# The first loads, warm-ups and last output tile of a gated mix of linear attention and a token MLP

## The chip, the core and the metric

The kernel runs on one core of one Trainium2 chip. A core has engines that run side by side, each with its own queue of instructions: TensorE (matmuls, PE in the profile; its weight loads are PEld), VectorE (DVE), ScalarE (ACT), GpSimd (POOL) and SyncE (SP), which here only issues DMAs. The metric is the device time of the kernel in microseconds (us).

## The reference, cut to what matters

```
x: 2048 x 512, 32 heads of 16; everything in bf16
g  = sigmoid(sum(x * gate_w))                     one number per token
q, k, v = x @ wqkv                                phi(t) = where(t > 0, t + 1, exp(t)) + 1e-6
kv = sum over tokens of phi(k) v^T                per head, and z = sum of phi(k)
a  = (phi(q) @ kv) / (phi(q) . z + 1e-6) @ wo
h  = layernorm(x)
u  = gelu(h^T @ w1 + b1)                          w1 mixes the 2048 tokens into 1792
b  = (u @ w2 + b2)^T
out = g * a + (1 - g) * b
```

## The kernel before, in words

The 2048 tokens are 16 tiles of 128 (`NT`), the 512 features 4 chunks of 128 (`ND`). `xs` holds x with tokens on partitions, `xT` holds it with features on partitions, `hs` the normalised x, `pk` phi of k, `pqT` phi of q transposed.

The order of instructions on each engine is the order in which the code is written (`manual_schedule`); a wait is placed where an instruction needs another's result. PSUM is used as eight banks, taken in turn (`bank`). The stages are:

1. Loads and warm-ups. SP issues most DMAs one after the other; ACT issues the first two loads of the k weights (`load_wk`). `load_x` brings a tile of x as it lies, `load_xT` brings tiles through the transposing DMA. Meanwhile `warm_up` runs matmuls on a constant.
2. The k loop. Tiles 0 and 1 (`HEADS`) are not loaded transposed: TensorE transposes them against an identity (`transpose_part`), VectorE or ScalarE copies the result into `xT` (`copy_part`), and then `k_part` multiplies them with Wk, chunk by chunk. From tile 2 on `xT` comes from the transposing loads. `k_phi` applies phi (ScalarE, then VectorE twice). Four tiles later (`LAG`) `g_tile` accumulates x^T phi(k) over all tokens, which needs the plain tile of x. `ln_step` takes a tile's mean and variance on VectorE.
3. The first three blocks of h^T w1, with the q blocks between; then the remaining blocks of u, with the small matrices of the attention and the normalisers beside them.
4. The output loop: for each tile a product for the attention (`aps`), fourteen for the MLP (`yps`), the sum on VectorE and a store. The last tile is cut into pieces of columns, so that its first stores can leave early.

In stage 2 TensorE's order for the first two tiles is this:

```
for t in range(HEADS):
    for k0, k1 in ((0, 1), (1, 2), (2, ND)):
        transpose_part(t, k0, k1)
        copy_part(t, k0, k1, (t, k0) in ((0, 2), (1, 1)))
    k_part(0, range(2) if t == 0 else (2,))
k_part(1, range(2))
k_part(0, (3,))
```

All matmuls pass through the helper `mm`, so they share line 110; the tiles' names tell them apart: `wps` warm-ups, `pt` transposes, `kacc` k_part, `gacc` g_tile, `yps` the output. `load_x` is line 126, `load_wk` line 129, `load_xT` line 132, `ln_step` lines 233 and 234, the sum of the output line 501 and its store line 505.

Of the kernel before, what the change touches and what calls it, by code (L numbers as in the profile page):

```python
# [15 lines left out]
def kernel(  # L16
# [13 lines left out]
    nc = tc.nc  # L30
    P = nc.NUM_PARTITIONS
# [4 lines left out]
    X = A_x.flatten_outer_dims()  # L36
    O = out.flatten_outer_dims()
    S, D = X.shape
    F = B_w1.shape[1]
    NT = S // P  # L40
# [25 lines left out]
    def keep(shape, dtype, name):  # L66
        return persist.tile(shape, dtype, name=name, tag=name)

    def bank(name, dtype=FP32):
        return ps.tile([P, SC], dtype, name=name, tag="bank")  # L70

    xs = keep([P, NT, D], BF16, "xs")
    hs = keep([P, NT, D], BF16, "hs")
# [16 lines left out]
    ident = keep([P, P], BF16, "ident")  # L90
# [18 lines left out]
    def mm(o, lhsT, rhs, start, stop, **kw):  # L109
        nc.tensor.matmul(o, lhsT=lhsT, rhs=rhs, start=start, stop=stop, **kw)  # L110
# [14 lines left out]
    def load_x(q, t0, n):  # L125
        q.dma_start(out=xs[:, t0 : t0 + n, :], in_=x_view[:, t0 : t0 + n, :])

    def load_wk(q, k, n):
        q.dma_start(out=wk_sb[:, k : k + n, :], in_=wqkv_view[:, k : k + n, D : 2 * D])

    def load_xT(t0, n):
        nc.sync.dma_start(
            out=xT[:, :, t0 * P : (t0 + n) * P], in_=X[t0 * P : (t0 + n) * P, :], transpose=True
        )

    load_x(nc.sync, 0, 1)
    load_wk(nc.scalar, 0, 2)
    load_x(nc.sync, 1, 1)
    load_wk(nc.scalar, 2, 1)
    load_wk(nc.sync, 3, 1)  # L140
    for t in (2, 3, 4):
        load_xT(t, 1)
    nc.vector.memset(ones_f[:], 1.0)
# [3 lines left out]
        out=ident[:], in_=ident[:], compare_op=ALU.not_equal, fill=1.0, base=0,  # L147
# [5 lines left out]
        out=maskQ[:], in_=maskH[:].rearrange("p (a m) -> p m a", m=2), op=ALU.max, axis=AX.X  # L153
    )
    nc.gpsimd.memset(brow[:], 0.0)

    load_xT(5, 2)
    load_x(nc.sync, 2, 2)
    load_xT(7, 3)
# [15 lines left out]
    def load_small():  # L175
        nc.gpsimd.dma_start(out=brow[0:NF, :], in_=B_b1.rearrange("(f q) -> f q", q=P))
        nc.gpsimd.dma_start(out=brow[NF : NF + NT, :], in_=B_b2.rearrange("(f q) -> f q", q=P))
        nc.gpsimd.dma_start(
            out=gw_b[:], in_=gate_w.rearrange("(o d) -> o d", o=1).to_broadcast([P, D])
        )  # L180
# [3 lines left out]
    def warm_up(n, cols=SC):  # L184
        for _ in range(n):
            mm(wps[:, :cols], warm[:, 0:P], warm[:, :cols], True, True)

    act_warm = keep([P, 1], FP32, "act_warm")
    nc.scalar.activation(out=act_warm[:], in_=ones_f[:], func=ACT.Exp)
    warm_up(6)  # L190

    pts = {}

    def transpose_part(t, k0, k1):
        pt = pts[t, k0, k1] = bank("pt")
        for k in range(k0, k1):
            mm(pt[:, k * P : (k + 1) * P], xs[:, t, k * P : (k + 1) * P], ident[:], True, True)

    def copy_part(t, k0, k1, on_act):
        src = pts.pop((t, k0, k1))[:, k0 * P : k1 * P].rearrange("p (k s) -> p k s", k=k1 - k0)  # L200
        dst = xT[:, k0:k1, t * P : (t + 1) * P]
        if on_act:
            nc.scalar.activation(out=dst, in_=src, func=ACT.Copy)
        else:
            nc.vector.tensor_copy(out=dst, in_=src)  # L205
# [13 lines left out]
    def k_part(t, ks):  # L219
        if t not in kaccs:  # L220
            kaccs[t] = bank("kacc")
        for k in ks:
            mm(
                kaccs[t][:], xT[:, k, t * P : (t + 1) * P], wk_sb[:, k, :],
                k == 0, k == ND - 1,
            )

    def k_phi(t):
        phi(pk[:, t, :], kaccs.pop(t))

    def ln_stats(t):
        stats = work.tile([P, nc.vector.BN_STATS_DIM], FP32, name="stats", tag="stats", bufs=2)
        nc.vector.bn_stats(out=stats[:], in_=xs[:, t, :])  # L233
        nc.vector.bn_aggr(out=mv[:, t, :], in_=stats[:])  # L234

    def ln_rstd(g):
        s = slice(g * TPC, (g + 1) * TPC)
        nc.vector.tensor_scalar_add(out=veps[:, s], in0=mv[:, s, 1], scalar1=EPS)
        nc.gpsimd.tensor_tensor(out=rstd[:, s], in0=veps[:, s], in1=mhalf[:], op=ALU.pow)

    def ln_shift(g):
        s = slice(g * TPC, (g + 1) * TPC)
        nc.vector.scalar_tensor_tensor(  # L243
            out=nmr[:, s], in0=mv[:, s, 0], scalar=-1.0, in1=rstd[:, s],
            op0=ALU.mult, op1=ALU.mult,
        )

    def ln_apply(t):
        nc.scalar.activation(  # L249
            out=hs[:, t, :], in_=xs[:, t, :], func=ACT.Identity,  # L250
            scale=rstd[:, t : t + 1], bias=nmr[:, t : t + 1],
        )
# [3 lines left out]
    def g_tile(t):  # L256
        if not gacc:
            gacc.extend(bank("gacc") for _ in range(ND))
        for k in range(ND):
            mm(gacc[k][:], xs[:, t, k * P : (k + 1) * P], pk[:, t, :], t == 0, t == NT - 1)  # L260
# [15 lines left out]
    def ln_step(u):  # L276
        ln_stats(u)
        if u % TPC == TPC - 1:
            ln_rstd(u // TPC)
# [9 lines left out]
    k_phi(0)  # L289
    k_part(1, range(2, ND))  # L290
    k_phi(1)
    ln_step(0)
    ln_step(1)
    LAG = 4
    LN_LAG = 5
    APPLY = 10
    for t in range(HEADS, NT):
        k_part(t, range(ND))
        k_phi(t)
        if t >= LAG:  # L300
            g_tile(t - LAG)
        if t > LN_LAG + 1:
            ln_step(t - LN_LAG)
        if t == TPC - 1 + LN_LAG:
            load_small()
        if t >= APPLY:
            ln_apply(t - APPLY)
        if t in (TPC + LN_LAG, 2 * TPC + LN_LAG):
            ln_shift((t - LN_LAG) // TPC - 1)
# [73 lines left out]
    def den_block(c, j):  # L383
        seg = pqT[:, j, c * SC : (c + 1) * SC]
        pz = work.tile([P, SC], FP32, name="pz", tag="pz", bufs=2)
        nc.scalar.activation(out=pz[:], in_=seg, func=ACT.Copy, scale=zcol[:, j : j + 1])  # L386
        nc.vector.transpose(out=zT[:], in_=pz[:])  # L387
        den = work.tile([P, SC // HEAD], FP32, name="den", tag="den", bufs=1)
        nc.vector.tensor_reduce(  # L389
            out=den[:], in_=zT[:].rearrange("p (a d) -> p a d", d=HEAD), op=ALU.add, axis=AX.X  # L390
        )
        rd = work.tile([P, SC // HEAD], BF16, name="rd", tag="rd", bufs=1)
        with nc.allow_low_precision(reason="the normalizer is used in bf16"):
            nc.vector.reciprocal(out=rd[:], in_=den[:])
        rex = work.tile([P, SC], BF16, name="rex", tag="rex", bufs=1)
        nc.vector.transpose(  # L396
            out=rex[:].rearrange("p (a d) -> p a d", d=HEAD),
            in_=rd[:].unsqueeze(2).to_broadcast([P, SC // HEAD, HEAD]),
        )
        nc.vector.tensor_tensor(out=seg, in0=seg, in1=rex[:], op=ALU.mult)  # L400
# [42 lines left out]
    for j in range(NB0, NF):  # L443
        c, jj = divmod(j, FB)
        i = j - NB0
        acc = bank("uacc")
        for t in range(NT):
            if i == 2 and t < BRIDGE:
                for q in range(0, P, Q32):
                    c0 = jj * P + q  # L450
# [24 lines left out]
        out=gg[:], in0=gth[:], scalar1=0.5, scalar2=0.5, op0=ALU.mult, op1=ALU.add  # L475
    )
    nc.vector.tensor_scalar(
        out=c1[:], in0=gth[:], scalar1=-0.5, scalar2=0.5, op0=ALU.mult, op1=ALU.add
# [3 lines left out]
    for t in range(NT):  # L482
        c, tl = divmod(t, TPC)
        aps = bank("aps")
        for j in range(ND):
            mm(aps[:], pqT[:, j, t * P : (t + 1) * P], W2sb[:, j, :], j == 0, j == ND - 1)
        a_sc = work.tile([P, D], FP32, name="a_sc", tag="a_sc", bufs=2)
        nc.scalar.activation(  # L488
            out=a_sc[:], in_=aps[:], func=ACT.Identity,
            scale=gg[:, t : t + 1], bias=c2[:, t : t + 1],  # L490
        )
        for c0, W in ((0, 2 * P), (2 * P, P), (3 * P, P)) if t == NT - 1 else ((0, D),):
            cs = slice(c0, c0 + W)
            yps = bank("yps")
            for f in range(NF):
                mm(
                    yps[:, :W], w2c[c][:, f, tl * P : (tl + 1) * P], uT[:, f, cs],
                    f == 0, f == NF - 1,
                )
            ot = opool.tile([P, D], BF16, name="ot", tag="ot")  # L500
            nc.vector.scalar_tensor_tensor(  # L501
                out=ot[:, :W], in0=yps[:, :W], scalar=c1[:, t : t + 1], in1=a_sc[:, cs],
                op0=ALU.mult, op1=ALU.add,
            )
            (nc.scalar if t < 2 else nc.sync).dma_start(out=o_view[:, t, cs], in_=ot[:, :W])
        if t < NSC * ND - NDB:
            den_block(*divmod(t + NDB, ND))
# [30 lines left out]
```

## Time and profile before

| | us |
|---|---|
| median of 3 runs | 162.76 (162.43 to 162.89) |
| time of the profiled execution | 162.26 |
| its span, first to last instruction | 160.6 |
| TensorE busy | 155.9 |
| VectorE busy | 124.3 |
| ScalarE busy | 72.7 |

The profile is one execution. Its span lies inside its time; the rest is start and end of the launch. A line of the timeline has the start in us from the span's start, the duration in us, the engine, the line of the code and what is written from what; a letter q behind an engine's name means that the engine issued a DMA. The chain is followed back from the last instruction to what released it, and printed in order of time. A matmul's end is modelled, and neighbouring matmuls overlap in the records; the starts are what to compare. The granted clock of TensorE is 1.00 for the whole span.

### The profile page before, as it was taken

To read this page: it belongs to the slowest core of one execution; us is meant where nothing else is said; L and a number is where in the kernel's file an instruction comes from. 1 tells how busy PE (TensorE), PEld (TensorE's weight loads), DVE (VectorE), ACT (ScalarE), POOL (GpSimd) and SP (SyncE) were. 2 spreads that over 40 slices of the span, in tenths; PEclk is the share of its full clock that TensorE was granted. 3 is DMA by queue.
4 is the path that set the end of the run, shared out by engine and by line. 5 is a ranking of instruction groups with operands and counts; after the bars stand their busy time and mean duration, and the time that the engine had idled before them with its cause. 6 is when DMAs were issued, how large, how long until landed. Compare 5 with 4: busy or idle time off the path is not lost.

```text
span 160.6 us, 2228 instructions
## 1 busy us (share of the span) xinstructions
PE 155.9 (97%) x822; PEld 72.5 (45%) x836; DVE 124.3 (77%) x274; ACT 72.7 (45%) x113; POOL 7.3 (5%) x17
## 2 busy tenths in 40 slices
PE   7999999999999999999999999999999999999993
PEld 2444444444444445444444444444444444444462
DVE  1599999769999998756999999676999999711122
ACT  3543486654978393059873320237333442111110
POOL 3000332002010000000000000000000000000000
PEclk9999999999999999999999999999999999999999
DMA  5699999999970007600930679401000001110001
GB/s 168 150 231 262 328 352 329 354 349 348 336 171 0 0 0 257 204 0 4 356 101 2 213 244 306 151 33 37 33 33 33 33 33 58 48 61 33 33 33 33
DMA packets 29929, 23.07 MB, mean 144 GB/s; under 512 B 8384, under 2 KB 29888, under 8 KB 29920
## 3 DMA queue, kind: packets, MB, share of 16 engines
q1 hardware_dynamic: 29104, 22.15, 45.2%
q10 hardware_dynamic: 704, 0.66, 1.2%
q0 software_dynamic: 112, 0.14, 0.4%
q8 instruction: 6, 0.10, 0.3%
q14 instruction: 3, 0.02, 0.0%
HBM read 19.01 MB, written 2.10 MB: 131 GB/s over the span
## 4 chain that ended last, share of the span: by engine, by line
PE 84%; DVE 13%; issue 1%; ACT 0%
PE yps L110 30%; PE uacc L110 24%; PE kacc L110 9%; PE gacc L110 9%; PE aps L110 9%; DVE pqT L213 6%; DVE zacc L274 3%; DVE stats L233 2%; DVE e L210 2%; PE wps L110 2%; PE qacc L110 1%; DVE mv L234 1%; ACT e L209 0%; PE kvps L110 0%; PE w2ps L110 0%
## 5 line engine op out<-in xcount | busy, mean ns | idle before, releaser
L110 PE MATMUL uacc<-hs,w1c 128*128 128x512 bf16 (+1 forms) x227 | 50.8, 379 | 0.4 <-issue 0.2
L110 PE MATMUL yps<-uT,w2c 128*128 128x512 bf16 (+2 forms) x247 | 50.8, 355 | 0.3
L110 PEld LDWEIGHTS <-w2c 128*128 128x128 bf16 x252 | 23.6, 98 | 25.2
L110 PEld LDWEIGHTS <-w1c 128*128 128x128 bf16 (+1 forms) x233 | 21.8, 98 | 26.0 <-issue 0.2
L488 ACT ACTIVATE a_sc<-aps,c,gg 128x512 f32<-128x512 f32 x16 | 12.4, 775 | 31.2 <-PE aps L110 15.5
L501 DVE SCALAR_TENSOR_TENSOR ot<-yps,c,a_sc 128x512 bf16<-128x512 f32 (+2 forms) x18 | 12.3, 688 | 15.3 <-PE yps L110 11.7
L322 ACT ACTIVATE uT<-uacc,bcol 128x512 bf16<-128x512 f32 x14 | 9.3, 686 | 17.5 <-PE uacc L110 17.4
L110 PE MATMUL qacc<-xT,wq_sb 128*128 128x512 bf16 x64 | 16.4, 379 | 0.1
L110 PE MATMUL aps<-W2sb,pqT 128*128 128x512 bf16 x63 | 16.4, 379 | 0.1
L110 PE MATMUL kacc<-wk_sb,xT 128*128 128x512 bf16 x63 | 15.9, 379 | 0.2 <-DVE xT L205 0.2
L387 DVE STREAM_TRANSPOSE zT<-pz 128x512 f32<-128x512 f32 x16 | 11.3, 705 | 6.0 <-ACT pz L386 6.0
L110 PE MATMUL gacc<-pk,xs 128*128 128x512 bf16 x63 | 15.7, 379 | 0.1
L249 ACT ACTIVATE hs<-xs,nmr,rstd 128x512 bf16<-128x512 bf16 x16 | 12.8, 805 | 2.3 <-DVE nmr L243 2.3
L209 ACT ACTIVATE e<-kacc 128x512 bf16<-128x512 f32 x16 | 9.4, 594 | 9.7 <-PE kacc L110 8.5
L386 ACT ACTIVATE pz<-pqT,zcol 128x512 f32<-128x512 bf16 x16 | 11.4, 715 | 4.8 <-DVE ot L501 4.7
L209 ACT ACTIVATE e<-qacc 128x512 bf16<-128x512 f32 x16 | 9.5, 594 | 7.7 <-PE qacc L110 7.7
L396 DVE STREAM_TRANSPOSE rex<-rd 128x512 bf16<-128x512 bf16 x16 | 11.4, 711 | 0.6
L213 DVE SCALAR_TENSOR_TENSOR pqT<-qacc,e 128x512 bf16<-128x512 f32 x16 | 11.1, 692 | 0.6
L213 DVE SCALAR_TENSOR_TENSOR pk<-kacc,e 128x512 bf16<-128x512 f32 x16 | 11.1, 692 | 0.6
L389 DVE TENSOR_REDUCE den<-zT 128x32 f32<-128x512 f32 x16 | 11.0, 686 | 0.6
L210 DVE TENSOR_SCALAR e<-e 128x512 bf16<-128x512 bf16 x32 | 9.0, 282 | 2.5 <-ACT e L209 2.5
L233 DVE BATCH_NORM_STATS2 stats<-xs 128x6 f32<-128x512 bf16 x16 | 10.9, 683 | 0.0
(58 smaller groups left out, 96.2 us busy)
## 6 DMA issues: line engine op xcount, KB each, us to landing
w2c<-in_B_w_dram SPq DMA_DIRECT2D x8, 896.0 KB, 5.7
w1c<-in_B_w_dram SPq DMA_DIRECT2D x3, 2048.0 KB, 14.0
out_dram<-ot SPq DMA_DIRECT2D x13, 128.0 KB, 1.7
xs<-in_A_x_dram SPq DMA_DIRECT2D x1, 1024.0 KB, 6.6
w1c<-in_B_w_dram SPq DMA_DIRECT2D x1, 1024.0 KB, 15.3
xs<-in_A_x_dram SPq DMA_DIRECT2D x1, 512.0 KB, 5.0
wq_sb<-in_A_wqkv_dram SPq DMA_DIRECT2D x1, 512.0 KB, 5.6
wv_sb<-in_A_wqkv_dram SPq DMA_DIRECT2D x1, 512.0 KB, 12.3
```

Of the source, the lines that this page charges most:

```text
L110: nc.tensor.matmul(o, lhsT=lhsT, rhs=rhs, start=start, stop=stop, **kw)
L209: nc.scalar.activation(out=e[:], in_=acc[:], func=ACT.Exp)
L210: nc.vector.tensor_scalar(out=e[:], in0=e[:], scalar1=1.0, scalar2=PHI_EPS, op0=ALU.min, op1=ALU.add)
L213: nc.vector.scalar_tensor_tensor(out=dst, in0=acc[:], scalar=0.0, in1=e[:], op0=ALU.max, op1=ALU.add)
L233: nc.vector.bn_stats(out=stats[:], in_=xs[:, t, :])
L249: nc.scalar.activation(out=hs[:, t, :], in_=xs[:, t, :], func=ACT.Identity, scale=rstd[:, t : t + 1], bias=nmr[:, t : t + 1],)
L386: nc.scalar.activation(out=pz[:], in_=seg, func=ACT.Copy, scale=zcol[:, j : j + 1])
L387: nc.vector.transpose(out=zT[:], in_=pz[:])
L389: nc.vector.tensor_reduce(out=den[:], in_=zT[:].rearrange("p (a d) -> p a d", d=HEAD), op=ALU.add, axis=AX.X)
L396: nc.vector.transpose(out=rex[:].rearrange("p (a d) -> p a d", d=HEAD), in_=rd[:].unsqueeze(2).to_broadcast([P, SC // HEAD, HEAD]),)
L488: nc.scalar.activation(out=a_sc[:], in_=aps[:], func=ACT.Identity, scale=gg[:, t : t + 1], bias=c2[:, t : t + 1],)
L501: nc.vector.scalar_tensor_tensor(out=ot[:, :W], in0=yps[:, :W], scalar=c1[:, t : t + 1], in1=a_sc[:, cs], op0=ALU.mult, op1=ALU.add,)
```

## The change

The first tile of x for the transposes is loaded as 64 partitions with two consecutive tokens each (rows of 2 KB) into a corner of `hs` that is not used until later. It is transposed in eight products 64 wide, one for each chunk and each of the two tokens, and `copy_part` puts the two interleaved halves in place. The plain load of tile 0, which `g_tile` and `ln_step` need, is issued on SP after three transposing loads, and `ln_step(0)` moves behind tile 5 of the k loop. Of the Wk loads, chunks 1 and 2 go first on ACT, chunk 0 second on SP, chunk 3 second on ACT; tile 1 of x is the third load of SP. The warm-ups are four matmuls of 512 columns and one of 384 instead of six of 512. The last output tile is cut into 384 and 128 columns instead of 256, 128 and 128.

```diff
-    load_x(nc.sync, 0, 1)
-    load_wk(nc.scalar, 0, 2)
+    xp = hs[: P // 2, 0:2, :]
+    nc.sync.dma_start(out=xp, in_=X[0:P, :].rearrange("(p i) d -> p i d", i=2))
+    load_wk(nc.scalar, 1, 2)
+    load_wk(nc.sync, 0, 1)
+    load_wk(nc.scalar, 3, 1)
     load_x(nc.sync, 1, 1)
-    load_wk(nc.scalar, 2, 1)
-    load_wk(nc.sync, 3, 1)
     for t in (2, 3, 4):
         load_xT(t, 1)
...
+    load_x(nc.sync, 0, 1)
     load_xT(5, 2)
...
-    warm_up(6)
+    warm_up(4)
+    warm_up(1, 384)
...
         for k in range(k0, k1):
-            mm(pt[:, k * P : (k + 1) * P], xs[:, t, k * P : (k + 1) * P], ident[:], True, True)
+            if t == 0:
+                for i in range(2):
+                    c = k * P + i * (P // 2)
+                    mm(
+                        pt[:, c : c + P // 2], xp[:, i, k * P : (k + 1) * P],
+                        ident[: P // 2, : P // 2], True, True,
+                    )
+            else:
+                mm(pt[:, k * P : (k + 1) * P], xs[:, t, k * P : (k + 1) * P], ident[:], True, True)
...
+        if t == 0:
+            src = src.rearrange("p k (i s) -> p k i s", i=2)
+            dst = dst.rearrange("p k (s i) -> p k i s", i=2)
...
-    ln_step(0)
     ln_step(1)
...
+        if t == LN_LAG:
+            ln_step(0)
...
-        for c0, W in ((0, 2 * P), (2 * P, P), (3 * P, P)) if t == NT - 1 else ((0, D),):
+        for c0, W in ((0, 3 * P), (3 * P, P)) if t == NT - 1 else ((0, D),):
```

## The prediction

> **What bounds the kernel now.** I read the page first, then the chain that ended last, then the first ten microseconds on each queue and engine.
>
> ```profile
> span 160.6 us, 2228 instructions
> PE 155.9 (97%) x822; PEld 72.5 (45%) x836; DVE 124.3 (77%) x274; ACT 72.7 (45%) x113; POOL 7.3 (5%) x17
> ...
> PE 84%; DVE 13%; issue 1%; ACT 0%
> ```
>
> TensorE is busy for 97% of the span. The chain, in order of time, shows where it isn't:
>
> ```profile
> 0.85 2.72 PE wps L110 x6
> ...
> 4.06 0.60 PE kacc L110 x2
> 4.66 0.22 PE pt L110 x4
> 4.89 0.22 PE kacc L110
> 5.10 0.00 issue
> 5.11 3.84 PE kacc L110 x17
> 8.95 0.86 PE gacc L110 x4
> ...
> 154.69 3.10 PE yps L110 x42
> ```
>
> From 5.11 us to the last matmul at 157.8 us TensorE has no hole worth naming (the VectorE stretch of the chain from 33.8 to 55.5 us runs level with it). So whatever moves that 5.11 moves the end by as much, and beyond it only the tail counts. What sets the 5.11 is seen in the loads of the first microseconds (source, queue, KB, us from issue to landing, each issue asked for by itself):
>
> ```profile
> wk_sb<-in_A_wqkv_dram ACTq DMA_DIRECT2D x1, 256.0 KB, 3.1
> xs<-in_A_x_dram SPq DMA_DIRECT2D x1, 128.0 KB, 2.3
> ...
> xs<-in_A_x_dram SPq DMA_DIRECT2D x1, 128.0 KB, 3.0
> wk_sb<-in_A_wqkv_dram ACTq DMA_DIRECT2D x1, 128.0 KB, 3.3
> ...
> wk_sb<-in_A_wqkv_dram SPq DMA_DIRECT2D x1, 128.0 KB, 3.3
> ```
>
> SP issues at 0.81, 1.27 and 1.73, ACT at 0.81 and 1.30. Issue plus landing gives five slots: first SP load 3.1, first ACT load 3.9, second SP load 4.3, second ACT load 4.6, third SP load 5.0. They land in the order of issue, 0.3 to 0.8 apart. The DMA engines' share in steps of 0.5 us says why:
>
> ```profile
> 1.80:2.30 0.50, 0.50 (x3) 0.16 (x2) 0.16 (x1) 0.48 (x1) 0.38 (x2) 1.00 0.54 147
> 2.30:2.80 0.50, 0.50 (x2) 0.15 (x1) 0.00 (x0) 0.50 (x1) 0.00 (x0) 1.00 0.87 287
> 2.80:3.30 0.50, 0.50 (x2) 0.10 (x1) 0.00 (x0) 0.49 (x2) 0.00 (x0) 1.00 1.07 373
> ```
>
> (The last two columns are the DMA share and GB/s.) From 2.8 us the 16 engines are full. The front is a queue of 768 KB through a full pipe, and the order in it is what the change alters.
>
> **The change, part by part.**
>
> *The order of the first loads.* Before, the slots carry x tile 0, Wk chunks 0 and 1, x tile 1, Wk chunk 2, Wk chunk 3. After, they carry x tile 0, Wk 1 and 2, Wk 0, Wk 3, x tile 1. The bytes in each slot are the same; x tile 1 goes from the third slot (4.3) to the fifth (5.0), Wk 0 from the second (3.9) to the third (4.3). TensorE's order is kept: two k_part products of tile 0, then the four transposes of tile 1, then the rest. So Wk 3, now early, gains nothing: its product stands behind the transposes of tile 1, and so does everything else on TensorE. Wk 0 at 4.3 lets the two products run from 4.3 to about 4.75 instead of 4.06 to 4.5, which ends before x tile 1 is there. What decides is x tile 1. Today its weights load at 4.32 and its transposes start at 4.50, when the two products are through:
>
> ```profile
> 4.32 0.39 PEld L110 LDWEIGHTS <-xs 128*128 128x128 bf16 x4
> 4.50 0.39 PE L110 MATMUL pt<-ident,xs 128*128 128x128 bf16 x4
> ```
>
> After, they start at landing plus 0.05. Bounds of that landing: no x load before came sooner than 2.3 after its issue, so 1.73 + 2.3 = 4.03 at the least; the fifth slot as it is, 5.04; and 5.3 if the new first load takes 0.3 longer. I take 5.0, since the queue in front of it holds the same 640 KB. Slip: 5.05 - 4.50 = 0.55 us, with ends of -0.4 and +0.85. The steps behind the transposes (copies, products) are the same, so 5.11 becomes about 5.66.
>
> *The first tile as 64 rows of 2 KB.* The trace has no such load. It can help by at most what the engines leave idle between 1.8 and 2.8: 0.46 x 0.5 + 0.13 x 0.5 = 0.30 us, which would bring every slot forward by as much (x tile 1 at 4.74, slip 0.29). It can hurt by 0.3, if half the partitions draw on half the engines (147 GB/s at a share of 0.54 is that picture). I take about 0.05 of gain, already in the 5.0. The Trainium skill, "SBUF — State Buffer", section "Door 1: The DMA port swizzle", speaks against this part: partitions 0 to 63 reach only 8 of the 16 DMA ports, about 218 GB/s instead of 436. An estimate from that page is 0.3 us more for these 128 KB; the sum below would then be 0.8 instead of 0.5.
>
> *Its transposes and copies.* Eight products 64 wide instead of four 128 wide, and copies that write every second column. Today 0.87 us pass from the weight load at 3.19 to the first k_part product at 4.06. Even with x tile 0 no earlier and four more transposes at the 0.13 of today's slow ones (0.53 for 4), that makes 3.19 + 0.87 + 0.53 = 4.59 and the two products end at 5.03. The cover is x tile 1 at 5.05; if that came at 4.74, up to 0.25 would show.
>
> *Warm-ups.* 4.75 instead of 6 matmuls of 0.45 (2.72 / 6): 0.57 us off TensorE before 3.6 us, where it would wait for loads anyway. Gain zero. The risk is the rate: warm-ups go at 0.45 us each, the k_part products at 0.226 (3.84 / 17), and the step falls between 3.6 and 4.1 us after some 2.8 us of unbroken work. The granted clock in the rows says 1.00 on both sides, so only durations show it. After the change TensorE pauses twice before 5 us. I take no cost; the far end is five products and four transposes at the slow rate, 5 x 0.22 + 4 x 0.05 = 1.3 us. The Trainium skill, "TensorE: Matmul & The Clock Gate", Part 1, ties the rate to about 3.4 us of sustained activity; by that rule the thinned front would run slow for longer, and as an estimate the sum would be nearer 1.
>
> *The plain load of tile 0, now on SP behind three transposing loads.* It takes the issue place at 6.16, and costs SP the 0.42 of a like issue plus a gap, so all later SP loads go 0.45 later. First in line is the transposing load for tiles 5 and 6:
>
> ```profile
> 6.16 1.30 SPq L132 DMA_TRANSPOSE xT<-in_A_x_dram  x1
> ...
> xT<-in_A_x_dram SPq DMA_TRANSPOSE x1, 3.1
> ...
> 8.57 0.75 PEld L110 LDWEIGHTS <-xs 128*128 128x128 bf16 x4
> 9.43 0.74 PEld L110 LDWEIGHTS <-xT 128*128 128x128 bf16 x4
> ```
>
> It lands at 6.16 + 3.1 = 9.26 and its first weight load is at 9.43: 0.17 of slack. After: 6.61 + 3.1 = 9.71, against 9.43 + 0.55 = 9.98, so it hides under the slip, with 0.27 to spare. But it is a floor: if x tile 1 came early, this load would hold TensorE at a slip of 0.3 all the same. The plain tile itself is wanted by g_tile(0), at 8.57 + 0.55 = 9.12; it lands at 6.16 + 2.3 = 8.46, at worst 6.16 + 3.3 = 9.46, 0.34 late. I take the former, as the queue has drained by then. Behind these, tiles 2 and 3 of x (issue 7.50, landing 3.0 later, wanted at 12.02) and the rest have over half a microsecond to spare.
>
> *ln_step(0) moved* from before phi of tile 2 to behind phi of tile 5: one bn_stats and bn_aggr, 0.68 + 0.18. VectorE works through from 6.59 to 14.76 and meets its input again only at tile 7 (14.79), so the pair is done within the same stretch. Zero; 0.86 if it ended after that point.
>
> *The tail.* 28 instead of 42 matmuls for the same 7168 columns. 42 take 3.10, 14 of 512 columns take 3.02, so an extra matmul costs 0.003: 14 fewer save 0.04. The sum of the 384 wide piece on VectorE is near 0.62 (0.484 at 256, 0.752 at 512) and starts 0.78 before the last piece is ready; its store is issued before the last one. The last 128 columns and their store are as before.
>
> **Sum:** +0.55 - 0.04 = +0.51 us on the profiled execution's 162.26, so 162.77. The median of the runs shown, 162.76, lies 0.5 above that profile, so the same sum on the median is 163.3 us.
>
> **Rivals.** (1) Not slower: the 2 KB rows land so much sooner that all slots move up. The place is x tile 1, the price 0.3: landing at 4.74, slip 0.29, then the floor of the tiles 5 and 6 load at 0.3. That gives 163.0. It decides if x tile 1 lands before 4.95. For it: the idle DMA share at 1.8 to 2.8. Against: the pipe is full from 2.8 on.
> (2) The matmul rate stays low into the dense stretch: 0.4 to 1.3 more, 163.7 to 164.6. For it: 1.25 warm-ups fewer and two pauses. Against: the step came well before 5 us, and most of the work ahead of it remains.
> (3) Faster: SP's loads don't queue behind ACT's, and x tile 1 lands near 4.03. Then the load for tiles 5 and 6 holds TensorE unless it, too, lands in 2.7 (the shortest transposing load seen), at 9.3: slip -0.1, 162.6. Against: the five slots land in strict order today.
>
> **How the numbers follow.** A difference of 0.3% (0.49 us) is about what a measurement tells from no change. Main case 0.50, with slips of 0.4 to 0.85 (163.1 to 163.6), about a third of it under 0.49; rival (1) 0.25; rival (2) 0.15; rival (3) 0.10, partly within 0.3%. So slower 0.53, same 0.40, faster 0.07. The range 162.6 to 164.1 goes from rival (3) to the low half of rival (2).
>
> **What would show it.** The chain's dense k_part stretch starts near 5.65 instead of 5.11; the weight load of x tile 1 waits for its DMA to about 5.0; the load for tiles 5 and 6 lands near 9.7, with no wait there; the last stretch on TensorE falls by 0.04. I am wrong if x tile 1 lands before 4.5, if the weight load for tile 5 or for g_tile(0) waits long, or if k_part products after 5.6 take 0.4 us.

## The result and the profile after

The changed kernel takes 181.51 us (median of 5 runs, 181.31 to 182.16), the kernel before 162.53 us. The ratio is 1.117, with a 95% interval of 1.115 to 1.120. The forecast was 163.3 us: the direction came true, the size and the cause were missed. The profiled execution took 182.16 us.

The page after, its span, engines and chain:

```profile
span 180.4 us, 2206 instructions
...
PE 157.6 (87%) x811; PEld 72.1 (40%) x825; DVE 124.3 (69%) x273; ACT 72.8 (40%) x113; POOL 7.3 (4%) x17
...
PE 86%; SPq 7%; DMA 4%; issue 1%; DVE 0%; DVEq 0%
```

The work is nearly the same, TensorE 157.6 us against 155.9; its share fell from 97% to 87%. Two owners are new in the chain: SP's queue and the DMAs. In order of time (start, duration in us):

```profile
11.14 2.72 SPq L132
...
14.54 7.49 DMA xT<-in_A_x_dram
...
22.15 0.31 DVE xT L219
...
22.51 0.61 PE kacc L110
23.12 0.43 PE pt L110 x4
23.55 5.24 PE kacc L110 x18
```

The k_part stretch that began at 5.11 us begins at 23.55. Ahead of it stands a copy on VectorE (line 219, `copy_part`), and ahead of the copy a DMA into `xT` that was issued at 14.54 and landed at 22.03. That is the load of tiles 13 to 15, the last of the seven transposing loads. The table of waits names the two copies that stood still, and TensorE behind them (total, times, longest):

```profile
ACT xT L217 <- DMA xT<-in_A_x_dram: 18.8, 1, 18.8
...
DVE xT L219 <- DMA xT<-in_A_x_dram: 16.5, 1, 16.5
PE kacc L110 <- DVE xT L219: 16.2, 1, 16.2
```

These copies write tile 0 of `xT`; the loads write tiles 2 to 15. No element is shared. The copy of chunk 0 didn't wait, only those of the later chunks. The front of the timeline shows that, and a second surprise:

```profile
0.81 1.00 ACTq L129 DMA_DIRECT2D wk_sb<-in_A_wqkv_dram  x2
...
0.81 0.58 SPq L137 DMA_DIRECT2D hs<-in_A_x_dram  x1
...
5.01 0.44 PEld L110 LDWEIGHTS <-hs 64*128 64x128 bf16 x8 [2.79 <-DMA hs<-in_A_x_dram]
5.02 0.60 PE L110 MATMUL pt<-ident,hs 64*128 64x64 bf16 x8 [1.99 <-DMA hs<-in_A_x_dram]
5.34 0.30 DVE L219 CAST xT<-pt 128x128 bf16<-128x128 f32 x1 [3.10 <-PE pt L110]
```

The first tile as 64 rows of 2 KB was ready for TensorE at 5.0 us, where the tile of 128 rows had been at 3.19. Its issue on SP took 0.58 us, where the load before took 0.40.

### The profile page after: what moved, and what is told of

Same layout as the page of the kernel before. It is cut to its first block, busy times and chain, and to the rows that moved or that the text cites. A ratio compares the mean times of both kernels' runs of the same rounds, so it can differ in the third digit from the quotient of the medians.

```text
span 180.4 us, 2206 instructions
## 1 busy us (share of the span) xinstructions
PE 157.6 (87%) x811; PEld 72.1 (40%) x825; DVE 124.3 (69%) x273; ACT 72.8 (40%) x113; POOL 7.3 (4%) x17
## 4 chain that ended last, share of the span: by engine, by line
PE 86%; SPq 7%; DMA 4%; issue 1%; DVE 0%; DVEq 0%
PE uacc L110 27%; PE yps L110 27%; PE kacc L110 8%; PE gacc L110 8%; PE aps L110 8%; PE qacc L110 7%; SPq L132 5%; DMA xT<-in_A_x_dram 4%; SPq L126 2%; PE kvps L110 0%; SPq L137 0%; SPq L129 0%; PE pt L110 0%; PE w2ps L110 0%; DVE ot L516 0%
## 5 line engine op out<-in xcount | busy, mean ns | idle before, releaser
L110 PEld LDWEIGHTS <-w2c 128*128 128x128 bf16 x238 | 22.8, 98 | 25.9
L110 PE MATMUL kacc<-wk_sb,xT 128*128 128x512 bf16 x62 | 17.7, 413 | 16.3 <-DVE xT L219 16.2
L110 PEld LDWEIGHTS <-xT 128*128 128x128 bf16 x64 | 6.7, 104 | 25.0 <-DVE xT L219 17.2
L219 DVE CAST xT<-pt 128x128 bf16<-128x128 f32 (+1 forms) x4 | 1.3, 330 | 20.5 <-DMA xT<-in_A_x_dram 16.5
## 6 DMA issues: line engine op xcount, KB each, us to landing
w1c<-in_B_w_dram SPq DMA_DIRECT2D x3, 2048.0 KB, 13.5
```

## The experiments

The leading theory after the result: the copies of tile 0 wait for the transposing loads because their destination is now written as a split pattern (even and odd columns). The rival: the new loads and their order starve TensorE, and the wait is a sign of that. The smaller parts of the change were then measured one by one. Each ratio below is to the kernel before on the same chip, with its 95% interval. Each trace is of one execution.

**e1: the changed kernel without the split destination.**

```diff
-                    c = k * P + i * (P // 2)
-                    mm(pt[:, c : c + P // 2], xp[:, i, ...], ident[: P // 2, : P // 2], True, True)
+                    po = pt[:, k * P : (k + 1) * P].rearrange("p (s i) -> p i s", i=2)
+                    mm(po[:, i, :], xp[:, i, ...], ident[: P // 2, : P // 2], True, True)
...
-        if t == 0:
-            src = src.rearrange("p k (i s) -> p k i s", i=2)
-            dst = dst.rearrange("p k (s i) -> p k i s", i=2)
```

> The changed kernel, with one thing undone: the two halves of tile 0 are put in place by the transposing matmuls (every second column of PSUM) instead of by the copies, whose destination in xT is then one plain run per chunk, as before. Theory (the copies of chunks 1 to 3 wait for the transposing loads of tiles 5 to 15 because of the way their destination is written): that wait goes, TensorE's dense stretch starts near 6.5 us instead of 23.5, and the time is 163.5 to 165.5 us, the rest over 162.5 being the first tile's late landing (4.97 us in the changed kernel) and some slow matmuls. Rival (the first loads themselves, the 64 rows of 2 KB and their order, starve TensorE): little changes, over 175 us.

Measured: 166.15 us (165.05 to 166.69), ratio 1.022 (1.019 to 1.024). Its chain from the start:

```profile
0.81 4.03 DMA hs<-in_A_x_dram
4.83 0.05 issue
4.88 1.03 PE pt L110 x8
5.91 0.97 PE kacc L110 x2
6.88 0.43 PE pt L110 x4
7.30 4.32 PE kacc L110 x18
```

The wait is gone, and 15.4 of the 19.0 us with it. The 3.4 us that remain begin with the load of the first tile, 4.03 us from issue to landing. They are a little over the theory's range. Part of them is the price of this edit itself: the same eight products took 0.60 us in the changed kernel, where each writes 64 neighbouring PSUM columns, and take 1.03 here, where each writes every second one. The matmul rate was low in both.

**e2: the kernel before with the split pattern alone.**

```diff
         dst = xT[:, k0:k1, t * P : (t + 1) * P]
+        if t == 0:
+            src = src.rearrange("p k (s i) -> p k i s", i=2)
+            dst = dst.rearrange("p k (s i) -> p k i s", i=2)
```

> The kernel before, with one thing added: the copies of tile 0 name source and destination as even and odd columns, so that the same numbers go to the same places through a split pattern. Loads, warm-ups, transposes and tail are those of before. Theory (the split destination alone brings the wait): the second copy waits until the load for tiles 13 to 15 lands, near 21.8 us in the profile before, and the time is 179 to 182 us. Rival (the loads are the cause): 162.5 to 163 us.

Measured: 180.42 us (2 runs), ratio 1.109 (1.104 to 1.113). The same numbers go to the same places, and no load was touched. In the timeline the copies of chunk 0 and of chunk 1:

```profile
3.71 0.30 DVE L208 CAST xT<-pt 128x128 bf16<-128x128 f32 x1 [1.48 <-PE pt L110]
...
20.34 0.30 DVE L208 CAST xT<-pt 128x128 bf16<-128x128 f32 x1 [16.34 <-DMA xT<-in_A_x_dram]
```

This settles the cause: the pattern alone costs 17.7 us, and the rival falls.

**e5: the changed kernel with its late loads written behind the copies.** The statements from the load of tiles 10 to 12 on move in the code to behind the loop over `HEADS`; SP's order of issue stays.

> The changed kernel, with the loads from the one for tiles 10 to 12 on (and all weights behind it) written behind the transposes and copies of tiles 0 and 1, so that no copy can be made to wait for them. Theory (a copy waits for every transposing load written ahead of it): the wait now ends when the load for tiles 7 to 9 lands, 11.9 us instead of 22.0 in the changed kernel's profile, and the time falls by about 10, to 170.5 to 172.5 us. Rival (the loads starve TensorE): unchanged or later, 181 to 184.

Measured: 173.84 us (2 runs), ratio 1.068 (1.064 to 1.072). The chain:

```profile
9.01 4.78 DMA xT<-in_A_x_dram
13.82 0.05 DVEq L207
13.87 0.05 issue
13.92 0.31 DVE xT L207
```

The wait now ends with the load of tiles 7 to 9, the last one written ahead of the copies. It landed at 13.79 us. The 11.9 of the forecast was a misreading: in the changed kernel that load lands 4.4 us after its issue at 9.06, at 13.5; at 11.9 lands the plain load of tiles 2 and 3. From 22.0 to 13.8 is 8.2 us, and the time fell by 7.7. A copy with a split destination waits for the transposing loads that stand before it in the code.

It works the other way round too. The loads now written behind the copies had to wait for them; SP issued the one for tiles 10 to 12 only at 14.38 us, where the changed kernel issued it at 11.14:

```profile
SPq L132 <- DVE xT L207: 3.2, 1, 3.2
```

**e3: the order of the first loads alone,** on the kernel before.

```diff
-    load_wk(nc.scalar, 0, 2)
-    load_x(nc.sync, 1, 1)
-    load_wk(nc.scalar, 2, 1)
-    load_wk(nc.sync, 3, 1)
+    load_wk(nc.scalar, 1, 2)
+    load_wk(nc.sync, 0, 1)
+    load_wk(nc.scalar, 3, 1)
+    load_x(nc.sync, 1, 1)
```

> The kernel before, with the order of the first loads alone changed: Wk chunks 1 and 2 and then 3 on ACT, x tile 0 (128 rows as before), Wk 0 and x tile 1 on SP. The prediction's first step: x tile 1 lands in the fifth slot near 5.0 us, TensorE's dense stretch starts at 5.66 instead of 5.11, and the time is 0.5 us more, 163.0 (0.15 to 0.8 more). Rival (what is on SP overtakes what is on ACT): 162.4 to 162.6.

Measured: 163.12 us (eleven runs at 162.84 to 163.73, one at 165.32) against 162.74, ratio 1.0025 (1.0008 to 1.0041). The chain has what the prediction described:

```profile
1.73 3.50 DMA xs<-in_A_x_dram
5.23 0.05 issue
5.27 0.40 PE pt L110 x4
5.67 0.21 PE kacc L110
5.89 0.01 issue
5.89 3.84 PE kacc L110 x17
```

The dense stretch starts 0.78 us later than in the profile before (5.89 against 5.11), but the medians differ by only 0.4. The kernel before ran at 162.26 to 163.43 here, and its profiled execution (162.26) stands at the fast end of that.

**e4: the 64 rows alone** (e1 with the load order, warm-ups and tail of before).

```diff
     nc.sync.dma_start(out=xp, in_=X[0:P, :].rearrange("(p i) d -> p i d", i=2))
-    load_wk(nc.scalar, 1, 2)
-    load_wk(nc.sync, 0, 1)
-    load_wk(nc.scalar, 3, 1)
-    load_x(nc.sync, 1, 1)
+    load_wk(nc.scalar, 0, 2)
+    load_x(nc.sync, 1, 1)
+    load_wk(nc.scalar, 2, 1)
+    load_wk(nc.sync, 3, 1)
...
-    warm_up(4)
-    warm_up(1, 384)
+    warm_up(6)
...
```

> The load order, warm-ups and tail of before; from the change only the first tile as 64 rows of 2 KB (put in place by the transposing matmuls, as in e1_plain_write), the plain load of tile 0 behind three transposing loads, and ln_step(0) moved. Theory (the 64-row load itself lands late, 4.84 us in e1_plain_write against 3.14 before): transposes of tile 0 start near 4.9, and the time is 164 to 166 us, most of e1's 166.15. Rival (it lands late only since Wk 0 stands behind it in the queue of SP): it lands by 3.2 us, 162.5 to 163.2.

Measured: 165.62 us (164.17 to 166.06), ratio 1.015 (1.011 to 1.020). The tile lands 3.85 us after its issue and is transposed from 4.70 us on. So most of what e1 kept is here too (2.9 of 3.4 us), and the chain begins with this load. The runs lie in two groups, two at 164.2 and four at 165.5 to 166.1. The profiled one is of the slower group, and in it the products behind the late tile are slow as well (eighteen in 5.21 us; seventeen took 3.84 before).

**e8 and e9: what makes that load late.** In both, ScalarE's table load stands ahead of its Wk loads; e8 is e4 so altered, e9 the kernel before.

```diff
+    nc.vector.memset(ones_f[:], 1.0)
+    act_warm = keep([P, 1], FP32, "act_warm")
+    nc.scalar.activation(out=act_warm[:], in_=ones_f[:], func=ACT.Exp)
     load_wk(nc.scalar, 0, 2)
```

> e4_rows_alone with ScalarE's table load and first activation put ahead of its two Wk loads, so that these are issued near 2.3 us instead of 0.8 and the 64-row load has no other load beside it at first. Only the landing of the first tile is read. Theory (ACT's load gets in front because the 64-row load's issue takes longer, 0.58 against 0.40): it lands by 3.2 us, 2.4 or less after its issue. Rival (a load to 64 partitions is slow by itself): 4 us after its issue or more, as in e1.

> The kernel before with the same move of ScalarE's table load; the partner of e8_rows_no_company with 128 rows of 1 KB. Only the landing of the first tile is read. Both theories: 2.0 to 2.3 us after its issue, 3.1 us or earlier.

The move did less than meant: ACT issued its Wk loads at 0.98 us, beside the table load, not at 2.3. Even so the 64-row tile got ahead. The last number of a line is the us from issue to landing; first e4, then e8:

```profile
wk_sb<-in_A_wqkv_dram ACTq DMA_DIRECT2D x1, 256.0 KB, 3.2
hs<-in_A_x_dram SPq DMA_DIRECT2D x1, 128.0 KB, 3.9
```

```profile
wk_sb<-in_A_wqkv_dram ACTq DMA_DIRECT2D x1, 256.0 KB, 3.2
hs<-in_A_x_dram SPq DMA_DIRECT2D x1, 128.0 KB, 2.6
```

And the tile of 128 rows in e9:

```profile
DMA to landing us min/median/max: 2.1/2.1/2.1
```

In e4 ACT's load lands at 4.0 us and the tile at 4.65; in e8 the tile lands at 3.4 and ACT's load at 4.2. With 0.17 us more of a start, the tile lands in 2.6 us instead of 3.9 to 4.2. So about 1.3 us of its lateness is order: its issue ends at 0.81 + 0.58 = 1.39, and the first of ACT's two ends at 1.29 in the changed kernel but at 1.44 in e8. About 0.5 us is the form itself, against 128 rows under the same conditions. Neither the theory's 2.4 nor the rival's 4 was met; each had a part of it. The Trainium skill, "SBUF — State Buffer", section "Door 1: The DMA port swizzle", says that partitions 0 to 63 reach half the ports; the estimate from it was 0.3 us, in the same direction as the 0.5.

**e10: e1 with nine warm-ups of 512 columns,** so that TensorE works until the first tile is there.

```diff
-    warm_up(4)
-    warm_up(1, 384)
+    warm_up(9)
```

> e1_plain_write with nine warm-ups of 512 columns instead of four and one of 384, so that TensorE works until about 4.7 us, when the first tile lands. Rival (2) of the prediction (the matmul rate stays low after the pause): the matmuls from 4.9 us on go at the fast rate, the dense stretch starts about 1 us earlier, and the time falls from 166.15 to 164.5 to 165.4 us. Otherwise (the pause costs nothing): no change, 166.

Measured: median 164.06 us, ratio 1.013 (1.008 to 1.018), but in two groups: four runs at 163.8 to 164.1 and two at 166.0 to 166.2. In the profiled run, one of the slower, the matmul rate had not risen by 7.4 us, although TensorE had worked from 0.84 us on with one pause of 0.16:

```profile
5.00 1.03 PE pt L110 x8
6.03 0.97 PE kacc L110 x2
7.00 0.43 PE pt L110 x4
7.43 5.26 PE kacc L110 x18
```

Eighteen products in 5.26 us are part slow, part fast; before, seventeen took 3.84. At 0.43 us for a slow one (the spacing of the warm-ups) and 0.22 for a fast one, six or seven were slow, which puts the step near 10 us. The groups lie 2.1 us apart, about what a slow rate up to there costs. No run of the faster group was profiled, so that it had the fast rate from the start is inferred. Of the six runs, more warm-up brought four below all of e1's and left two in e1's range.

**e6, e7, e11, e12: the small parts.** e6 cuts the last tile into 384 and 128 columns, e7 shortens the warm-ups, e12 does both, each on the kernel before.

> The kernel before with the last tile cut into 384 and 128 columns. The prediction's term: 0.04 us less, seen in the last stretch of TensorE alone (3.10 to 3.06); the time is 162.4 to 162.8 us, not to be told from before. Rival (the sum over 384 columns holds up the last piece): 0.1 to 0.3 more.

> The kernel before with four warm-ups of 512 columns and one of 384. The prediction's term: zero, with a risk that the matmul rate steps up later. At best the transposes of tile 0 start at 3.2 instead of 3.36 us and the dense stretch 0.15 earlier, 162.4 to 162.8; if the slow rate lasts into the k loop, 0.4 to 1.3 more, 163.1 to 164.

> The kernel before with the two small parts of the change that touch no load: the shorter warm-ups and the tail of 384 and 128. If both terms hold, 0.04 to 0.2 us less than before, 162.3 to 162.7; if the matmul rate steps up later, 163.1 to 164.

| | median, us | ratio to before | interval |
|---|---|---|---|
| e6, tail | 163.01 | 1.0015 | 0.9999 to 1.0032 |
| e7, warm-ups | 163.39 | 1.0021 | 0.9998 to 1.0044 |
| e12, both | 162.76 | 1.0010 | 0.9990 to 1.0031 |

None can be told from the kernel before (162.76). In e6 the last stretch on TensorE is 28 matmuls in 3.07 us, as costed (3.06), and from its end to the end of the span 2.8 us pass as before, so the wider sum holds nothing up. e7 falls in two groups again, five runs at 162.25 to 162.78 and seven at 163.36 to 163.70. Its profiled run is of the second: the transposes start at 2.96 instead of 3.36, as hoped, and the slow rate then eats the gain:

```profile
3.81 1.01 PE kacc L110 x2
4.82 0.43 PE pt L110 x4
5.25 4.77 PE kacc L110 x18
```

But the late step is not the mark of the shorter warm-ups. The profiled run of e6 has it too, with the loads and warm-ups of before:

```profile
4.06 1.03 PE kacc L110 x2
5.09 0.43 PE pt L110 x4
5.52 4.21 PE kacc L110 x18
```

And the kernel before has runs above 163.1 us as well: nine of its 35, against three of twelve in e6, seven in e7 and five in e12. That shorter warm-ups make the late step more frequent is suggested by these counts, not shown.

e11 is the plain load of tile 0 alone: 128 rows go first into the free corner of `hs`, and the plain load and `ln_step(0)` stand where the change puts them.

```diff
-    load_x(nc.sync, 0, 1)
+    xp = hs[:, 0, :]
+    nc.sync.dma_start(out=xp, in_=X[0:P, :])
...
+    load_x(nc.sync, 0, 1)
     load_xT(5, 2)
...
-    ln_step(0)
     ln_step(1)
...
```

> The kernel before with the extra load alone: tile 0 is first loaded in 128 rows of 1 KB into the free corner of hs and transposed from there, its plain load stands on SP behind three transposing loads, and ln_step(0) is moved. The prediction's floor: the load for tiles 5 and 6 lands near 9.7 instead of 9.26, its weight load waits 0.27 to 0.5 us, and the time is 162.9 to 163.2 us. Rival (the queue catches up): 162.4 to 162.7.

Measured: 163.15 us, ratio 1.0024 (1.0010 to 1.0037). The load for tiles 5 and 6 holds TensorE:

```profile
8.62 0.75 PEld L110 LDWEIGHTS <-xs 128*128 128x128 bf16 x4
...
10.25 0.33 PEld L110 LDWEIGHTS <-xT 128*128 128x128 bf16 x3 [0.89 <-DMA xT<-in_A_x_dram]
```

## Why the prediction was wrong, point by point

**The step that failed** is "Its transposes and copies". It costed the new copies by their work alone (0.87 us and four more transposes) and found cover for them. It did not ask what a copy with a new destination pattern would wait for. Seven transposing loads also write `xT`, and they stand ahead of the copies in the code. The wait was 16.5 us, and e2 shows that the pattern alone brings 17.7 us. The work itself was small: the eight products took 0.60 us where four had taken 0.53. No rival held the wait: the sum and two of the rivals turned on when data lands, the third on the matmul rate, none on a wait between instructions that share no data. Why the pattern is taken for an overlap is inferred, not shown. In a row of `xT` the chunks lie one behind another. Tile 0 of chunk 0 lies before the first column of every load, and its copy did not wait; tile 0 of chunks 1 to 3 lies between a load's first and last column, and those copies did. That is what a test by extent, instead of by element, would do.

**"The first tile as 64 rows of 2 KB"** was the second failure. The bounds were 0.3 us either way; the tile came 1.8 later (3.19 to 5.01 for its weight load). The sum counted bytes and engine shares and took SP's issue for unchanged. The issue grew from 0.40 to 0.58, which let ACT's 256 KB go first, and the form cost 0.5 more. The idea that the 64 rows could land sooner had nothing for it in any run.

**The front as the place that decides** was right. TensorE is dense from its late start to the end, and nothing downstream gave the delay back.

**The order of the first loads** held: 0.55 us of slip forecast; in e3 0.4 by the medians and 0.78 by the trace. Tile 1 of x landed at 5.23 instead of 5.0. In the changed kernel it landed at 2.06 + 3.9 = 5.96, since the two issues ahead of it on SP took 0.58 and 0.56 us; the wait of the copies hid that. So the forecast's "slower" came true by a cause that it did not have, and is no credit to it.

**The plain load as a floor** held in kind and was small: a slip of 0.3 forecast; in e11 0.4 by the medians, 0.8 by the trace (10.25 against 9.43). The extra issue took 0.58 us instead of 0.42 and the transposing load behind it 3.42 to land instead of 3.1.

**Warm-ups** at zero with a risk above it, and rival (2): right in kind. The risk showed in seven runs of twelve of e7, at about 1.1 us from group to group, and in the two groups of e10, but also in e6 and in the kernel before, whose warm-ups are the full six.

**The tail** was right to 0.01 us, and too small to time. **ln_step(0)** was not separated; in e11 it runs without a gap from 13.00 us on, and VectorE's one new wait there (0.60 us, at 15.41) is for ScalarE.

So of the 19.0 us, 15.4 went with the split destination (e1 against the changed kernel). The other 3.4 of e1 come mostly from the 64-row load (transposes from 4.88 us instead of 3.36) and from the slow rate behind it, and about 0.4 from e1's own write into every second column. How much the lateness adds to the slow rate is not separated. No part of the change was found to be a gain, and no version run here beats the kernel before.

## What to carry to other kernels

When an edit changes how an operand is written, list everything else that writes or reads that tile, and look at what the instruction now waits for before costing its work. A view that splits a dimension can cost a false dependency on writes to other parts of the tile, earlier and later ones; put the permutation where the tile has no other writer (here PSUM, where it cost 0.43 us of TensorE). When loads race, the time of the issue itself can decide who goes first: 0.18 us more on one queue let the other's load pass. And before a small part is given credit or blame, look at how much the kernel before scatters by itself.

## What was not expected of the hardware

As the first load of SP, 64 partitions with 2 KB each took 0.58 us to issue against 0.40 for 128 with 1 KB, and landed in 2.6 us against 2.1 in a like place. The form isn't all that sets the issue: 128 rows of 1 KB took 0.58 behind a transposing load in e11.

Where a product 64 columns wide writes decided its time. While the rate was low, eight took 0.60 us in the changed kernel and in e5, each into 64 neighbouring PSUM columns, and 1.03 in e1, e4, e8 and e10, each into every second column.

The step of the matmul rate does not come at a fixed time: between 3.6 and 4.1 us in the profile before, near 6 us in e6 with the same loads and warm-ups, near 10 us in e10 in spite of more work before it. The Trainium skill, "TensorE: Matmul & The Clock Gate", Part 1, describes the activity window as free-running, so that the step varies from run to run; e6 against the profile before, and the two groups of e10 and of e7, agree with that, and with a rule by amount of warm-up alone they would not.
